# Loading V and storing the output four heads at a time in a grouped-query attention kernel

## The chip, the cores and the metric

The kernel runs on one core of a Trainium2 chip. The metric is the device time of one execution in microseconds. The engines are named as in the profile: PE is TensorE's matrix unit (PEld its weight load), DVE is VectorE, ACT is ScalarE, POOL is GpSimd, and SP is SyncE, which issues every DMA of this kernel. The core's DMA work is done by 16 DMA engines side by side. Each DMA is spread over all 16, and each engine ends its share with an increment of a semaphore, so that a DMA has landed when its semaphore has risen by 16.

## The reference

```python
B, Hq, Hkv, Sq, Sk, D = 16, 32, 8, 16, 2048, 128          # q, k and v are bfloat16

def reference(q, k, v):
    rep = Hq // Hkv                                        # 4 query heads share one K and V
    k = jnp.repeat(k, rep, axis=1)
    v = jnp.repeat(v, rep, axis=1)
    scores = jnp.einsum("bhqd,bhkd->bhqk", q, k) * D ** -0.5
    p = _softmax(scores, axis=-1)
    return jnp.einsum("bhqk,bhkd->bhqd", p, v)
```

There are 16 x 8 = 128 K/V heads. Each has K and V of 2048 x 128 (512 KB each) and serves 4 x 16 = 64 query rows. All of K and V, 134 MB, is read once, and 2 MB of output is written.

## The kernel before, in words

The 128 heads are taken in 64 *pairs* (numbered p, two heads with 128 query rows together, which fill the 128 partitions) and in 32 *quads* (numbered n, two pairs). Every engine runs one straight program written out at build time, and semaphores order the engines against each other.

For each pair the data goes this way. VectorE transposes K in blocks, two instructions a step (`kt`, L355). PE multiplies with the transposed queries into PSUM (`S`, L304 and L260), always for one half of the keys of both pairs of a quad. VectorE scales the scores out of PSUM into `Sneg`, of which there are three buffers, and takes their minimum on the way (L377), and a small instruction (L385) joins the minima of the two halves. ScalarE takes the exponential into `P` and sums the rows (L417). PE transposes `P` (`PT`, L316), ScalarE copies it out of PSUM (L427), and PE multiplies it with V (`PV`, L334 for most pairs, L340 for the rest), four pairs behind the exponential (`PVLAG`). ScalarE divides by the row sums into `Osb` (`norm`, L440 and L444), and VectorE does so for the last five pairs (L398). The two lists `pe_prog` and `act_prog` fix the order on PE and ScalarE.

All transfers go through one queue, in the order of the `sync` program. Its loop counts steps t. A step with an even t asks for K of quad t/2: 2 MB, 16 KB in each partition, into one of three buffers; from the fourth on it waits until the buffer's last transpose is done. Each step asks for V of pair t - 6, or t - 7 from pair 48 on (`VLAG`, `VLATE`): 1 MB, which in each partition is 4 KB from each of two heads, into one of seven buffers. From the eighth on it waits for the PV of the pair seven before (`sem_pv`, L216). Then the step stores the output of pair t - 14 (`SLAG`), 128 rows of 256 bytes, after its normalisation (L235 to L238), from one of eight buffers. V of the last pair comes in two pieces (`LASTV`). Every eighth step a load of Q, 256 KB, comes first. SP executes this in order: a wait before one transfer also holds back those behind it.

The users of those transfers wait as follows. PV of a pair waits for the landing of its V (L322). A normalisation writes its buffer only after the store eight pairs before has landed (L396 on VectorE, L436 on ScalarE). VectorE's first transpose of a quad waits for K (L354).

POOL makes an identity and a mask at the start, through four small tensors of their own (L185 to L198), and later spreads the queries out for their transpose (L176).

Of the kernel before, what the change touches and what calls it, by code (L numbers as in the profile page):

```python
# [5 lines left out]
ACT = mybir.ActivationFunctionType  # L6
# [3 lines left out]
I32 = mybir.dt.int32  # L10

NK = 3
NV = 7
NKT = 2
NS = 3
NPT = 4
NO = 8
NQ = 2
NSTAGE = 3
VLAG = 6  # L20
VLATE = 48
PVLAG = 4
SLAG = 14
QLEAD = 7
# [10 lines left out]
def bass_standalone__gqa_softmax__sampling_kernel(  # L35
# [19 lines left out]
    sb = lambda name, shape, dt: ctx.enter_context(nc.sbuf_tensor(name, shape, dt))  # L55
    sem = lambda name: ctx.enter_context(nc.semaphore(name))

    iota_t = sb("iota_t", [128, 128], I32)
    ident4 = sb("ident4", [128, 128], F32)
    iota_m = sb("iota_m", [128, 4, 4], I32)  # L60
    lo_m = sb("lo_m", [128, 4, 4], F32)
    hi_m = sb("hi_m", [128, 4, 4], F32)
    mask = sb("mask", [128, 4], F32)
    Kn = [sb(f"Kn{i}", [128, 4 * J * 128], BF16) for i in range(NK)]
    Vb = [sb(f"Vb{i}", [128, 2, J, 128], BF16) for i in range(NV)]
    KT = [sb(f"KT{i}", [128, 2 * J * 64], F32) for i in range(NKT)]
    Qn = [sb(f"Qn{i}", [128, 8, 128], BF16) for i in range(NQ)]
    Q4 = sb("Q4", [128, 8, 2, 4, 64], BF16)
# [1 line left out]
    Sneg = [sb(f"Sneg{i}", [128, Sk], F32) for i in range(NS)]  # L70
    P = [sb(f"P{i}", [128, Sk // 2], F32) for i in range(2)]
    PT = [sb(f"PT{i}", [128, J // 2, 128], F32) for i in range(NPT)]
    Osb = [sb(f"O{i}", [128, 128], BF16) for i in range(NO)]
    nhalf = sb("nhalf", [128, 2, NP], F32)
    nbias = sb("nbias", [128, NP], F32)
    rowsum = sb("rowsum", [128, NP], F32)
    rrec = sb("rrec", [128, NP], F32)

    S_ps = ctx.enter_context(nc.psum_tensor("S_ps", [128, Sk], F32))
    ST_ps = ctx.enter_context(nc.psum_tensor("ST_ps", [128, NSTAGE * 512], F32))  # L80
# [1 line left out]

    sem_id = sem("sem_id")
    sem_k = [sem(f"sem_k{i}") for i in range(NK)]
    sem_v = [sem(f"sem_v{i}") for i in range(NV)]
    sem_vl = [sem(f"sem_vl{i}") for i in range(2)]
    sem_q = [sem(f"sem_q{i}") for i in range(NQ)]
    sem_o = [sem(f"sem_o{i}") for i in range(NO)]
# [92 lines left out]
    with nc.Block() as block:  # L181

        @block.gpsimd
        def _(gp):
            gp.iota(iota_m[:, :, :], [[-8, 4], [-32, 4]], base=0, channel_multiplier=1).then_inc(sem_id, 1)  # L185
            gp.iota(iota_t[:, :], [[1, 128]], base=0, channel_multiplier=-1).then_inc(sem_id, 1)
            gp.wait_ge(sem_id, 2)
            gp.tensor_scalar(ident4[:, :], iota_t[:, :], 0.0, None, op0=ALU.is_equal).then_inc(sem_id, 1)
            gp.tensor_scalar(lo_m[:, :, :], iota_m[:, :, :], 0.0, None, op0=ALU.is_ge).then_inc(sem_id, 1)
            gp.tensor_scalar(hi_m[:, :, :], iota_m[:, :, :], 8.0, None, op0=ALU.is_lt).then_inc(sem_id, 1)  # L190
            gp.wait_ge(sem_id, 5)
            gp.tensor_tensor(lo_m[:, :, :], lo_m[:, :, :], hi_m[:, :, :], op=ALU.mult).then_inc(sem_id, 1)
            for x in range(2):
                gp.wait_ge(sem_id, 6 + x)
                a = lo_m[:, :, :] if x == 0 else hi_m[:, :, :]
                w = 2 >> x
                dst = hi_m[:, :, 0:2] if x == 0 else mask[:, :].unsqueeze(2)
                gp.tensor_tensor(dst, a[:, :, 0:w], a[:, :, w:2 * w], op=ALU.add).then_inc(sem_id, 1)  # L198
            gp.wait_ge(sem_id, 8)
            for c in range(1, NQC):  # L200
                gp.wait_ge(sem_st, last_q[c - 1, 3] + 1)
                lay_q(gp, c)

        @block.sync
        def _(sp):
            def load_k(n):
                s = n % NK
                if n >= NK:
                    sp.wait_ge(sem_kt, 4 * (n - NK) + 4)
                sp.dma_start(Kn[s][:, :], kf[n]).then_inc(sem_k[s], 16)  # L210

            def load_v(p):
                s = p % NV
                if p >= NV:
                    sp.wait_ge(sem_pv, p - NV + 1)
                if p < NP - 1:  # L216
                    dst = Vb[s][:, :, :, :].rearrange("a g j d -> a g (j d)")
                    sp.dma_start(dst, vf[:, 2 * p:2 * p + 2, :]).then_inc(sem_v[s], 16)
                    return
                for x, (lo, hi) in enumerate(LASTV):  # L220
                    dst = Vb[s][:, :, lo:hi, :].rearrange("a g j d -> a g (j d)")
                    src = vf[:, 2 * p:2 * p + 2, 128 * lo:128 * hi]
                    sp.dma_start(dst, src).then_inc(sem_vl[x], 16)

            def load_q(c):
                s = c % NQ
                if c >= NQ:
                    sp.wait_ge(sem_q4, 4 * (c - NQ + 1))
                src = qf[1024 * c:1024 * (c + 1), :].rearrange("(a j) d -> a j d", j=8)
                sp.dma_start(Qn[s][:, :, :], src).then_inc(sem_q[s], 16)  # L230

            def store(p):
                s = p % NO
                if p < NP - NLATE:
                    sp.wait_ge(sem_nm, p + 1)  # L235
                else:
                    sp.wait_ge(sem_nl, p - (NP - NLATE) + 1)
                sp.dma_start(of[128 * p:128 * (p + 1), :], Osb[s][:, :]).then_inc(sem_o[s], 16)  # L238

            for t in range(NP + SLAG + 1):  # L240
                for c in range(NQC):
                    if t == max(0, 8 * c - QLEAD):
                        load_q(c)
                if t < NP and t % 2 == 0:
                    load_k(t // 2)
                if 0 <= t - VLAG < VLATE:
                    load_v(t - VLAG)
                if VLATE <= t - VLAG - 1 < NP:
                    load_v(t - VLAG - 1)
                if 0 <= t - SLAG < NP:  # L250
                    store(t - SLAG)
            for s in range(NO):
                sp.wait_ge(sem_o[s], 16 * (NP // NO))

        @block.tensor
        def _(pe):
# [15 lines left out]
            for op in pe_prog:  # L272
# [45 lines left out]
                elif op[0] == "PV":  # L318
                    _, p = op
                    pe.wait_ge(sem_ev, last_p[p, 1] + 1)  # L320
                    if p < NP - 1:
                        pe.wait_ge(sem_v[p % NV], 16 * (p // NV + 1))  # L322
                    if p >= NP - 4:
                        pe.wait_ge(sem_max, 2 * NP)
                    elif p >= 1:
                        pe.wait_ge(sem_nm, p)
                    pt = PT[p % NPT][:, :, :].bitcast(BF16).rearrange("p t (q e) -> p t e q", e=2)
                    for j in range(J):
                        if p == NP - 1:
                            for x, (lo, _) in enumerate(LASTV):  # L330
                                if j == lo:
                                    pe.wait_ge(sem_vl[x], 16)
                        if both_heads(p, NP):
                            ins = pe.matmul(  # L334
                                O_ps[:, 0:256], pt[:, j // 2, j % 2, :], Vb[p % NV][:, :, j, :],
                                start=(j == 0), stop=(j == J - 1),
                            )
                            continue
                        for g in range(2):
                            ins = pe.matmul(  # L340
                                o_ap(p)[64 * g:64 * (g + 1), :],
                                pt[:, j // 2, j % 2, 64 * g:64 * (g + 1)],
                                Vb[p % NV][:, g, j, :],
                                start=(j == 0), stop=(j == J - 1),
                                skip_group_check=True,
                            )
                    ins.then_inc(sem_pv, 1)

        @block.vector
        def _(dve):  # L350
# [41 lines left out]
            for p in range(NP - NLATE, NP):  # L392
                if p == NP - 2:
                    recip(NQD - 1)
                dve.wait_ge(sem_rec, p // 2 + 1)
                dve.wait_ge(sem_o[p % NO], 16 * (p // NO))  # L396
                dve.wait_ge(sem_pv, p + 1)
                dve.tensor_scalar(Osb[p % NO][:, :], o_ap(p), rrec[:, p:p + 1], None, op0=ALU.mult).then_inc(sem_nl, 1)  # L398

        @block.scalar  # L400
        def _(act):
            for op in act_prog:
# [28 lines left out]
                else:  # L431
                    _, p = op
                    act.wait_ge(sem_pv, p + 1)
                    act.wait_ge(sem_rec, p // 2 + 1)
                    if p >= NO:
                        act.wait_ge(sem_o[p % NO], 16 * (p // NO))  # L436
                    if both_heads(p, NP):
                        for g in range(2):
                            rows = slice(64 * g, 64 * (g + 1))
                            ins = act.activation(Osb[p % NO][rows, :], O_ps[rows, 128 * g:128 * (g + 1)], ACT.Copy,  # L440
                                                 scale=rrec[rows, p:p + 1])
                        ins.then_inc(sem_nm, 1)
                        continue
                    act.activation(Osb[p % NO][:, :], o_ap(p), ACT.Copy,  # L444
                                   scale=rrec[:, p:p + 1]).then_inc(sem_nm, 1)


# [26 lines left out]
```

## Time and profile before

| | |
|---|---|
| time, median of three runs | 341.38 us (341.27 to 341.43) |
| the profiled execution | 341.52 us, of which the span of the instructions is 339.7 us |
| DMA | 138.87 MB, mean 409 GB/s over the span |
| busy: PE, DVE, ACT, POOL | 303.7, 305.6, 254.5, 81.4 us |
| V loads: number, size, median from issue to landing | 63 of 1024 KB, 17.2 us (the last pair's two pieces apart) |
| K loads | 32 of 2048 KB, 19.1 us |
| stores | 64 of 32 KB, 16.2 us |
| Q loads | 8 of 256 KB, 14.9 us |

The page of the profile divides the span into 40 slices and shows for each the busy share of every engine in tenths; the DMA row is the mean of 16 DMA engines. The table of the queue counts packets, the single pieces that a DMA engine moves. The list of waits tells which engine stood idle, before which instruction, and what released it. The timeline of SP shows its issuing instructions: the second number is how long one issue took.

### The profile page before, as it was taken

The page shows a single profiled execution, that of the slowest core. Times are in us where ns is not written, and L with a number is a line of the kernel's source. Part 1 is how long each engine was busy: PE and PEld are TensorE (multiplying, and loading weights), DVE is VectorE, ACT ScalarE, POOL GpSimd, SP SyncE. Part 2 cuts the span into 40 slices and gives each one's busy share as a digit, 9 for nine tenths or more (in the row PEclk, how much of TensorE's full clock was granted, in tenths as well). Part 3 has the DMA queues.
Part 4 walks back from the last instruction along what each step waited for, and adds up shares of the span by engine and source line. Part 5 has one row for each costly group of instructions (what it writes and reads, how often), then busy time and mean ns, then how long its engine had stood idle before and what let it go on. Part 6 is the DMA issues. An engine that isn't in the chain of part 4 may idle for free.

```text
span 339.7 us, 7084 instructions
## 1 busy us (share of the span) xinstructions
PE 303.7 (89%) x3040; PEld 182.9 (54%) x2528; DVE 305.6 (90%) x457; ACT 254.5 (75%) x390; POOL 81.4 (24%) x40
## 2 busy tenths in 40 slices
PE   3467799999999999999989999799998999989895
PEld 3113365556655665566546655366555556546464
DVE  1989999999999999999999998899989999999931
ACT  3136878798878878888887887678886887887883
POOL 2840066000920057000750008400093000000000
PEclk9989999999999999999999999899999999999999
DMA  7999999999999999999999999999999999999994
GB/s 297 442 415 420 427 414 412 411 421 425 422 414 413 416 422 426 411 415 414 420 427 418 414 414 416 424 424 421 409 415 418 425 419 424 416 413 414 411 410 162
DMA packets 32688, 138.87 MB, mean 409 GB/s; under 512 B 10896, under 2 KB 11152, under 8 KB 28560
## 3 DMA queue, kind: packets, MB, share of 16 engines
q1 hardware_dynamic: 32656, 138.42, 99.7%
q8 instruction: 22, 0.36, 0.4%
q14 instruction: 10, 0.08, 0.1%
HBM read 136.31 MB, written 2.10 MB: 407 GB/s over the span
## 4 chain that ended last, share of the span: by engine, by line
DMA 35%; PE 35%; DVE 23%; ACT 3%; issue 2%; SPq 1%; ACTq 0%; DVEq 0%
DMA Kn<-in_k_dram 31%; DVE Sneg L377 12%; PE O_ps L334 11%; DVE KT L355 10%; PE S_ps L304 9%; PE S_ps L260 8%; PE ST_ps L316 5%; DMA Vb<-in_v_dram 4%; ACT P L417 2%; PE ST_ps L282 1%; PE O_ps L340 1%; ACT QT L408 1%; ACT O L440 0%; SPq L238 0%; ACT PT L427 0%
## 5 line engine op out<-in xcount | busy, mean ns | idle before, releaser
L355 DVE STREAM_TRANSPOSE KT<-Kn 128x1024 f32<-128x1024 f32 x128 | 151.0, 1218 | 10.9 <-DMA Kn<-in_k_dram 10.8
L377 DVE TENSOR_SCALAR_CACHE_REDUCE Sneg<-S_ps 128x1024 f32<-128x1024 f32 x128 | 150.7, 1209 | 7.9 <-PE S_ps L260 7.0
L417 ACT ACTIVATE P<-Sneg,nbias 128x2048 bf16<-128x2048 f32 x64 | 128.2, 2004 | 16.6 <-DVE nbias L385 15.5
L176 POOL TENSOR_SCALAR Q<-Qn,mask 128x1024 bf16<-128x1024 bf16 x28 | 79.2, 2847 | 175.0 <-DMA Qn<-in_q_dram 95.8
L304 PE MATMUL S_ps<-KT,QT 64*128 64x512 bf16 x512 | 102.7, 390 | 19.7 <-DVE Sneg L377 16.8
L260 PE MATMUL S_ps<-KT,QT 64*128 64x512 bf16 x512 | 102.5, 389 | 0.0
L334 PEld LDWEIGHTS O_ps<-Vb,PT 128*128 128x128 bf16 x672 | 62.6, 98 | 36.7 <-issue 29.8
L334 PE MATMUL O_ps<-Vb,PT 128*128 128x256 bf16 x672 | 81.1, 274 | 1.2 <-issue 1.2
L427 ACT ACTIVATE PT<-ST_ps 128x512 f32<-128x512 f32 x128 | 69.5, 594 | 11.9 <-PE ST_ps L316 10.8
L304 PEld LDWEIGHTS S_ps<-KT,QT 64*128 64x128 bf16 x512 | 27.4, 94 | 87.4 <-issue 75.9
L316 PE MATMUL ST_ps<-ident,P 128*128 128x128 f32 x512 | 67.6, 275 | 3.8 <-ACT P L417 3.7
L440 ACT ACTIVATE O<-O_ps,rrec 64x128 bf16<-64x128 f32 x84 | 30.5, 363 | 42.6 <-PE O_ps L334 42.0
L316 PEld LDWEIGHTS ST_ps<-ident,P 128*128 128x128 f32 x512 | 56.9, 141 | 9.5 <-ACT P L417 8.5
L282 PE MATMUL ST_ps<-ident,Q 128*128 128x128 f32 x128 | 20.4, 291 | 5.5 <-DVE Q L176 5.5
L340 PEld LDWEIGHTS O_ps<-Vb,PT 128*64 128x64 bf16 x576 | 16.7, 110 | 12.9 <-issue 12.9
L408 ACT ACTIVATE QT<-ST_ps 128x512 f32<-128x512 f32 x32 | 19.3, 602 | 5.4 <-PE ST_ps L282 5.4
L340 PE MATMUL O_ps<-Vb,PT 128*64 128x128 bf16 x576 | 19.5, 220 | 1.8 <-issue 1.3
L282 PEld LDWEIGHTS ST_ps<-ident,Q 128*128 128x128 f32 x128 | 16.4, 152 | 5.5 <-issue 5.5
L417 ACT ACTIVATION_READ_ACCUMULATOR P<-Sneg,nbias 128x1 f32 x64 | 12.2, 191 | 0.0
L377 DVE DVE_READ_ACCUMULATOR Sneg<-S_ps 128x1 f32 x128 | 10.6, 83 | 0.0
L444 ACT ACTIVATE O<-O_ps,rrec 128x128 bf16<-128x128 f32 x17 | 6.0, 354 | 3.0 <-PE O_ps L340 3.0
L398 DVE TENSOR_SCALAR O<-S_ps,rrec 128x128 bf16<-128x128 f32 x4 | 1.4, 350 | 6.5 <-PE S_ps L340 6.5
(19 smaller groups left out, 24.4 us busy)
## 6 DMA issues: line engine op xcount, KB each, us to landing
Kn<-in_k_dram SPq DMA_DIRECT2D x32, 2048.0 KB, 19.1
Vb<-in_v_dram SPq DMA_DIRECT2D x63, 1024.0 KB, 17.2
Qn<-in_q_dram SPq DMA_DIRECT2D x8, 256.0 KB, 14.9
out_dram<-O SPq DMA_DIRECT2D x64, 32.0 KB, 16.2
Vb<-in_v_dram SPq DMA_DIRECT2D x1, 768.0 KB, 13.1
Vb<-in_v_dram SPq DMA_DIRECT2D x1, 256.0 KB, 12.8
```

The costliest lines, as they stand in the source:

```text
L176: eng.tensor_scalar(Q4[:, :, :, r, :].rearrange("p j b x -> p (j b) x"), src, mask[:, r:r + 1], None, op0=ALU.mult,).then_inc(sem_q4, 1)
L260: return pe.add_instruction(mybir.InstMatmult(name=nc.get_next_instruction_name(), engine=mybir.EngineType.PE, ins=[pe.lower_ap(rhs), pe.l ...
L282: ins = pe.transpose(dst[:, 128 * j:128 * (j + 1)], src[:, 4 * x + j, b, :], ident4[:, :])
L304: ins = pe.matmul(s_ap, w, x, start=(acc == 0), stop=(acc == 3))
L316: ins = pe.transpose(dst[:, 128 * t:128 * (t + 1)], P[p % 2][:, 128 * x:128 * (x + 1)], ident4[:, :])
L334: ins = pe.matmul(O_ps[:, 0:256], pt[:, j // 2, j % 2, :], Vb[p % NV][:, :, j, :], start=(j == 0), stop=(j == J - 1),)
L340: ins = pe.matmul(o_ap(p)[64 * g:64 * (g + 1), :], pt[:, j // 2, j % 2, 64 * g:64 * (g + 1)], Vb[p % NV][:, g, j, :], start=(j == 0), stop ...
L355: dve.transpose(KT[n % NKT][:, :].rearrange("p (t b g e a) -> p e g t b a", t=J // 4, b=2, g=4, e=2)[:, e], Kn[Q % NK][:, :].bitcast(F32). ...
L377: dve.tensor_scalar(Sneg[p % NS][:, 1024 * x:1024 * (x + 1)].rearrange("p (t a m) -> p t a m", t=4, m=8), S_ps[:, 1024 * y:1024 * (y + 1)] ...
L417: act.activation(P[p % 2][:, :].bitcast(BF16), Sneg[p % NS][:, :], ACT.Exp, bias=nbias[:, p:p + 1], scale=-1.0, accum_out=rowsum[:, p:p + ...
L427: act.activation(PT[p % NPT][:, 4 * h:4 * (h + 1), :].rearrange("p t q -> p (t q)"), stage_ap(u), ACT.Copy,).then_inc(sem_ev, 1)
L440: ins = act.activation(Osb[p % NO][rows, :], O_ps[rows, 128 * g:128 * (g + 1)], ACT.Copy, scale=rrec[rows, p:p + 1])
```

## The change: V and output by quads

V is now loaded by quads for the first 24 quads (`VLATE = 24`, counted in quads): one DMA of 2 MB at the step at which the even pair was asked for, 4 KB from each of four heads in a partition. From quad 24 on V is still asked for by pairs, at the same steps as before. There are four V buffers of a quad in place of seven of a pair. A quad's load waits for the PV of the last pair that used the buffer, which is pair 2n - 7, the pair for which the even half waited before. Each buffer has two semaphores. A load of a quad raises only the first, and PV of both its pairs waits for that; with loads by pairs each pair has its own.

The output of both pairs of a quad is stored by one DMA of 64 KB up to quad 27 (`SLATE = 28`), at the step at which the odd pair was stored; from quad 28 on each pair is stored by itself. There are four output buffers of a quad in place of eight of a pair, and a normalisation of either pair waits for the store of the quad four before.

The larger V buffers take 64 KB of a partition instead of 56. The tensors for the identity and the mask at the start now lie inside the third `Sneg` buffer.

```diff
-NV = 7
+NV = 4
-NO = 8
+NO = 4
-VLATE = 48
+VLATE = 24
+SLATE = 28
...
-    Vb = [sb(f"Vb{i}", [128, 2, J, 128], BF16) for i in range(NV)]
+    Vb = [sb(f"Vb{i}", [128, 4, J, 128], BF16) for i in range(NV)]
...
-    Osb = [sb(f"O{i}", [128, 128], BF16) for i in range(NO)]
+    Osb = [sb(f"O{i}", [128, 2, 128], BF16) for i in range(NO)]
...
+    scratch = Sneg[NS - 1]
+    iota_t = scratch[:, 0:128].bitcast(I32)
...
             def load_v(p):
-                s = p % NV
-                if p >= NV:
-                    sp.wait_ge(sem_pv, p - NV + 1)
+                n, x = divmod(p, 2)
+                s = n % NV
+                if n < VLATE:
+                    if x == 1:
+                        return
+                    if n >= NV:
+                        sp.wait_ge(sem_pv, 2 * (n - NV) + 2)
+                    dst = Vb[s][:, :, :, :].rearrange("a g j d -> a g (j d)")
+                    sp.dma_start(dst, vf[:, 4 * n:4 * n + 4, :]).then_inc(sem_v[s][0], 16)
+                    return
+                sp.wait_ge(sem_pv, p - 2 * NV + 1)
                 if p < NP - 1:
-                    dst = Vb[s][:, :, :, :].rearrange("a g j d -> a g (j d)")
-                    sp.dma_start(dst, vf[:, 2 * p:2 * p + 2, :]).then_inc(sem_v[s], 16)
+                    dst = Vb[s][:, 2 * x:2 * x + 2, :, :].rearrange("a g j d -> a g (j d)")
+                    sp.dma_start(dst, vf[:, 2 * p:2 * p + 2, :]).then_inc(sem_v[s][x], 16)
                     return
...
             def store(p):
-                s = p % NO
+                n, x = divmod(p, 2)
+                s = n % NO
+                if n < SLATE:
+                    if x == 0:
+                        return
+                    sp.wait_ge(sem_nm, p + 1)
+                    dst = of[256 * n:256 * (n + 1), :].rearrange("(x r) d -> r x d", x=2)
+                    sp.dma_start(dst, Osb[s][:, :, :]).then_inc(sem_o[s], 16)
+                    return
...
                     if p < NP - 1:
-                        pe.wait_ge(sem_v[p % NV], 16 * (p // NV + 1))
+                        n, x = divmod(p, 2)
+                        if n < VLATE:
+                            pe.wait_ge(sem_v[n % NV][0], 16 * (n // NV + 1))
+                        else:
+                            pe.wait_ge(sem_v[n % NV][x], 16 * ((n if x == 0 else n - VLATE) // NV + 1))
...
-                dve.wait_ge(sem_o[p % NO], 16 * (p // NO))
+                dve.wait_ge(sem_o[p // 2 % NO], 16 * (p // 2 // NO))
...
-                    if p >= NO:
-                        act.wait_ge(sem_o[p % NO], 16 * (p // NO))
+                    if p >= 2 * NO:
+                        act.wait_ge(sem_o[p // 2 % NO], 16 * (p // 2 // NO))
```

## The prediction

> **What bounds the kernel now.** I read the page's slices first, then the queue table and the DMA issues, then the waits, the chain and the timeline of the queue and of the end. The slices and the queue table:
>
> ```profile
> PE   3467799999999999999989999799998999989895
> DVE  1989999999999999999999998899989999999931
> DMA  7999999999999999999999999999999999999994
> ...
> DMA packets 32688, 138.87 MB, mean 409 GB/s; under 512 B 10896, under 2 KB 11152, under 8 KB 28560
> ...
> q1 hardware_dynamic: 32656, 138.42, 99.7%
> ...
> Vb<-in_v_dram SPq DMA_DIRECT2D x63, 1024.0 KB, 17.2
> ...
> out_dram<-O SPq DMA_DIRECT2D x64, 32.0 KB, 16.2
> ```
>
> Three resources look full, but only the DMA row is full from the first slice to the last but one. Of the 32,656 packets on the queue, 8,192 are 256-byte output rows, 16,128 are 4 KB of V, 4,096 are 16 KB of K, and 2,704 = 169 x 16 are 4-byte completion marks: each of the 169 DMAs (32 K, 63 + 2 V, 8 Q, 64 stores) ends with one mark on each of 16 engines. That is the only count the change alters. (Times of single packets and marks here and below are from the trace's DMA records, which the queue table sums up.)
>
> Next, whether the queue ever runs dry. The sequencer that issues, in the middle:
>
> ```profile
> 244.10 1.27 SPq L210 DMA_DIRECT2D Kn<-in_k_dram  x1
> 245.41 0.44 SPq L218 DMA_DIRECT2D Vb<-in_v_dram  x1
> 245.89 0.47 SPq L238 DMA_DIRECT2D out_dram<-O  x1
> 246.40 6.52 SPq L218 DMA_DIRECT2D Vb<-in_v_dram  x1
> 252.96 1.72 SPq L238 DMA_DIRECT2D out_dram<-O  x1
> ```
>
> A free issue takes 0.4 to 0.5 us; here one takes 6.52 us, and the next starts the moment it ends. [...] The waits and the end:
>
> ```profile
> DVE KT L355 <- DMA Kn<-in_k_dram: 10.8, 11, 3.5
> ...
> 336.20 1.08 PE L340 MATMUL S_ps<-Vb,PT 128*64 128x128 bf16 x32 [0.96 <-DMA Vb<-in_v_dram]
> 337.43 0.35 DVE L398 TENSOR_SCALAR O<-S_ps,rrec 128x128 bf16<-128x128 f32 x1 [1.69 <-PE S_ps L340]
> ```
>
> VectorE waits for K, TensorE waits 0.96 us for the last V. From the completion marks K lands at 191.21, 201.32, 222.49 and 232.61, and its transposes start at 191.2, 201.3, 222.7 and 232.9: VectorE lives hand to mouth on the DMA stream. So the kernel is one ordered stream of packets, and its end is the stream's end on the slowest engine (336.8) plus the last PV, normalise and store.
>
> What a packet costs an engine, from the spacing of packet starts in the trace: 16 KB 607 ns, 4 KB 155 ns, 2 KB 80 ns, 256 B 14 ns, a mark 6 ns (recorded length 9 ns). A quad (K, two V, two stores) is 8 x 607 + 32 x 155 + 16 x 14 + 5 x 6 = 10.07 us; the marks of successive K loads (181.13, 191.21) give 10.08. VectorE needs about 9.4 us for the same quad (its transposes of two successive K loads ended at 100.2 and 109.6, with K well ahead), so the stream is the slower. There is no hidden gap per transfer of more than about 0.01 us.
>
> **The change, part by part.** The sum is made against the profiled execution, 341.52 us (339.7 span and 1.8 around it), which stands 0.14 above the median of 341.38.
>
> **Fewer transfers.** V goes from 65 DMAs to 24 + 15 + 2 = 41, stores from 64 to 28 + 8 = 36; 52 DMAs go, 52 marks on every engine. At the 6 ns spacing that is 0.31 us; at the recorded 9 ns, 0.47. The rest of the quad's measured time over its packets (10.08 to 10.13 against 10.07) is at most 0.06 us over 5 transfers, 12 ns each; two transfers less in 26 quads would then be worth up to 0.6 us more. From below: a mark that overlaps its neighbours wholly is worth 0. I take 0.35 us, nearest to the spacing, and keep 0 to 0.9.
>
> **Packets.** A partition's run in one head is 4 KB in DRAM before and after, and an output row 256 B; so data packets are the same in number and size. Their order changes: K, V, O, V, O becomes K, V, V, O, O. From the marks of the slowest engine, V behind K takes 2.54 us, V behind O 2.42, a store 0.16, K behind O 4.8. V behind V I see only before the first stores, at 24 to 29 us: 2.57. The second store of a pair has no row; by its packets it takes 0.11 to 0.13. A quad in the new order is 4.80 + 2.54 + 2.57 + 0.16 + 0.13 = 10.20 by these, and 10.07 - 0.01 = 10.06 by packet spacing alone; the old order gives 4.80 + 2.54 + 0.16 + 2.42 + 0.16 = 10.08. I take no change, because the packets are the same and the spacing is the nearer row (16 packets of 155 ns make 2.48, whatever stands ahead). For the range I keep +0.12 to -0.02 us in each of 24 quads, +2.9 to -0.5.
>
> **Does a transfer cost more than its packets?** On the empty queue at the end the last store takes 1.45 us from its issue (337.81) to its landing (339.26), but in the full queue a store adds 0.16 us to the stream: the latency is overlapped, and I count only the mark. [...]
>
> **SP.** It issues 52 instructions less, each 0.4 to 0.5 us when free. [...]
>
> **The added waits.** PV of an even pair now waits for the whole 2 MB. Before, PV of the even pairs 24 to 46 starts 0.9 to 2.9 us after the *odd* half has landed (the least, pair 34: PV at 208.00, odd half at 207.11). As the odd half moves ahead of a store (0.16) and sometimes of a Q load (0.54), it lands earlier still, so PV does not wait: 0. If that cover went, S of a later pair, queued behind PV on TensorE, would be late, then VectorE. Normalising an even pair now waits for the store of four heads, four quads back: the smallest margin by today's landings is 1.14 us (pair 62), 2.6 and more up to pair 58. Cost 0. The V load of a quad waits for the PV that its even half waited for, pair 2n - 7; it is free about 10 us before issue. [...]
>
> **The start.** The identity and mask constants move into Sneg's third buffer, which VectorE first writes at its fifth scaled eviction, at 23.9 us; POOL's 2.5 us of set-up lie before K lands at 8.8. Cost 0.
>
> **The end.** Late loads and stores stay as they are. TensorE's 0.96 us wait for the last V covers a stream that ends 0.35 earlier, so the gain reaches the last store whole: 341.52 - 0.35 = 341.17 against the profiled run, 341.38 - 0.35 = 341.03 against the median, 341.0.
>
> **The rivals.**
>
> **R1, the engines are freed of more than marks: faster.** The completion marks show that an engine falls behind by 1.2 to 1.4 us whenever one of the 22 16 KB instruction packets (q8) passes through it; the slowest engine got three (its marks jump at the packets of 34.5, 151.8 and 274.1 us) and lags the fastest by 4.9 us at the end. SP's shorter program may drop one 8 KB instruction fetch (q14, 0.31 us). With 52 x 14 ns = 0.73 for the marks and their surroundings, and with that fetch, 1.04 us: 340.3. For it: the 10.13 us quads. [...]
>
> **R2, four heads in one load read more slowly: slower.** V packets last 161 ns in the mean against a floor of 159; the mean of a single load reaches 165.7 (the one that starts at 297.8). If the walk over four heads, 512 KB apart in DRAM, or V directly behind V, holds the 24 big loads there, that is 24 x 32 x 4.4 ns = 3.4 us, 341.0 + 3.4 = 344.4; it decides from 0.5 ns a packet on. For it: the V loads before the first store, where no store parts them, average 163, which is 2 ns, 1.5 us, and 342.5. Against: the stores stay, only in twos, and from 67 us on V mostly lasts 159 to 163 behind K and behind a store alike; two heads already walk the same way. [...]
>
> **R3, PV or the normalise step waits after all: no change or slower.** It needs the 0.9 us margin to go; a wait of 1 us on TensorE in each quad would still be within VectorE's 0.7 us a quad of slack plus K's buffers, so the time stays near 341.4.
>
> **R4, nothing at all:** marks wholly overlapped, 341.4. [...]
>
> **R5, each transfer pays its latency:** 52 x 1.45 = 75 us; VectorE's 305.6 us of work, 8.8 before it and 3.7 of tail and launch behind it stop the fall at about 318. The back-to-back marks exclude it but for 0.01.
>
> **How the numbers follow.** A change of 0.2% (0.68 us) either way is about what a measurement of this kernel can tell from none. My forecast, 0.1 to 0.68 us gained, has 0.42, R4 0.10 and R3 0.03: together 0.55 within 0.2%. R1 with the good end of the order has 0.27 and R5 0.01: 0.28 faster by more. R2 has 0.17: slower by more. The likeliest time is 341.0. The range goes down to 340.0, past R1's 340.3, and up to 342.4, just under R2's milder form; about 0.06 is left out below and 0.13 above.
>
> **What the profile after would show.** Right: 31,824 packets on the queue (832 fewer), the DMA row as full as now, GB/s in the middle up by a tenth of a percent or so, V issues x24 of 2 MB, TensorE still waiting some 0.6 to 1 us for the last V. Wrong towards faster: K to K under 10.0 us, or a smaller lag of the slowest engine. Wrong towards slower: V packets at 163 ns or more, "PE O_ps <- DMA Vb" among the waits in mid-run, or ACT waiting for a store. The forecast fails if the cost of a transfer on an engine is not in its packets, or if the lag of the slowest engine changes.

## The result and the profile after

The kernel after takes 341.98 us (median of 22 runs) where the kernel before takes 341.40 (22 runs beside it): a ratio of 1.0020, with a 95% interval of 1.0013 to 1.0027. It is 0.58 us slower, and I had forecast a gain of 0.4. The time itself lies in the range I gave, on its other side. The profiled executions stand 0.33 apart, 341.85 against 341.52, their spans 340.1 against 339.7.

The page of the kernel after: the row of the 16 DMA engines, the packet count, the table of the queue, and the DMA issues.

```profile
span 340.1 us, 7030 instructions
...
DMA  7999999999999999999999999999999999999995
...
DMA packets 31856, 138.86 MB, mean 408 GB/s; under 512 B 10064, under 2 KB 10320, under 8 KB 27728
...
q1 hardware_dynamic: 31824, 138.42, 99.9%
...
Vb<-in_v_dram SPq DMA_DIRECT2D x24, 2048.0 KB, 23.3
...
out_dram<-O SPq DMA_DIRECT2D x28, 64.0 KB, 20.3
```

The queue moves the same 138.42 MB in 31,824 packets, 832 fewer: 52 marks on each of 16 engines, as the prediction counted. But the engines are busy for 99.9% of a span that is longer, not for less of it. Fewer packets took more time. The same is seen in the middle of the run, in the view by stretches from 160 to 260 us (the columns are busy times and counts of PE, PEld, DVE, ACT and POOL, the granted clock, the DMA share and GB/s). Before:

```profile
160.00:260.00 100.00, 93.56 (x901) 55.77 (x739) 92.37 (x138) 79.53 (x123) 33.93 (x12) 0.98 1.03 419
```

After:

```profile
160.00:260.00 100.00, 93.79 (x902) 56.16 (x743) 92.62 (x140) 79.21 (x123) 33.70 (x12) 0.98 1.03 418
```

The DMA share is the same and the rate falls from 419 to 418 GB/s, where I had looked for a small rise. The sequencer that issues, at the same place as before:

```profile
244.96 0.66 SPq L213 DMA_DIRECT2D Kn<-in_k_dram  x1
246.02 0.37 SPq L224 DMA_DIRECT2D Vb<-in_v_dram  x1
246.45 7.55 SPq L251 DMA_DIRECT2D out_dram<-O  x1
254.05 1.73 SPq L213 DMA_DIRECT2D Kn<-in_k_dram  x1
```

Issues are drawn out as before (6.52 us there): that of a store lasts 7.55 us here, where V's just ahead of it took 0.37. From the list of waits (us in total, times, longest):

```profile
DVE KT L378 <- DMA Kn<-in_k_dram: 11.0, 12, 3.6
```

From the timeline of the end:

```profile
336.54 1.08 PE L363 MATMUL S_ps<-Vb,PT 128*64 128x128 bf16 x32 [0.86 <-DMA Vb<-in_v_dram]
337.76 0.35 DVE L421 TENSOR_SCALAR O<-S_ps,rrec 128x128 bf16<-128x128 f32 x1 [1.59 <-PE S_ps L363]
```

VectorE's waits for K add up to 11.0 us against 10.8. No wait of PE for V and none of ACT for a store has joined the list in mid-run. The full list has one new row, VectorE idle for 2.7 us before a normalisation (L421), put down to a store. It shows no wait for a store: it is the normalisation of pair 61, at 333.78 us, and the store that it needed, of quad 26, had landed at 329.21 by the completion marks. What landed just before 333.78 was part of a later store on the same semaphore. POOL's idle time is only put down otherwise (125.3 us to Q instead of 95.8, 52.5 to PE instead of 79.2). The last V lands at 337.13 instead of 336.77, PE begins its last PV 0.34 later, and the last normalise comes 0.33 later. So the whole loss is in the stream.

Two numbers from the trace's DMA records are used below. One is the *stream time*: the completion mark of K of quad 26 less that of quad 6, each as the mean over the 16 engines, so that the lag of a single engine enters by a sixteenth. It covers twenty quads with 40 V loads of a pair; the first store follows K of quad 7, so 19 of the quads have stores, 38 of a pair. The other is the mean recorded length of the 4 KB packets in the first and second half of a quad's V (quads 4 to 23). The records do not name the engine, so these packets are counted off in the order of their starts, 256 to a half. In before and after the marks of one K lie 0.6 to 3.4 us apart in these quads, 1.8 and more from quad 5 on, so neighbouring halves mix, and the true differences may be larger. The stream time went from 207.41 to 207.92 us. The halves went from 161.7 and 160.6 ns to 161.7 and 164.0: the half that used to stand behind a store and now stands behind V became slower by 3.4 ns a packet.

### The profile page after: what moved, and what is told of

It reads as the page before. It is cut to its first block, busy times and chain, and to the rows that moved or that the text cites. A ratio compares the mean times of both kernels' runs of the same rounds, so it can differ in the third digit from the quotient of the medians.

```text
span 340.1 us, 7030 instructions
## 1 busy us (share of the span) xinstructions
PE 305.4 (90%) x3040; PEld 183.5 (54%) x2528; DVE 305.7 (90%) x457; ACT 254.6 (75%) x390; POOL 81.4 (24%) x40
## 3 DMA queue, kind: packets, MB, share of 16 engines
q1 hardware_dynamic: 31824, 138.42, 99.9%
## 4 chain that ended last, share of the span: by engine, by line
DMA 35%; PE 33%; DVE 22%; SPq 4%; ACT 3%; issue 2%; ACTq 0%; DVEq 0%
DMA Kn<-in_k_dram 32%; DVE Sneg L400 12%; PE O_ps L357 10%; DVE KT L378 10%; PE S_ps L323 8%; PE S_ps L279 8%; PE ST_ps L335 5%; DMA Vb<-in_v_dram 4%; SPq L241 2%; ACT P L440 2%; PE ST_ps L301 1%; SPq L251 1%; PE O_ps L363 1%; ACT QT L431 1%; ACT PT L450 0%
## 5 line engine op out<-in xcount | busy, mean ns | idle before, releaser
L179 POOL TENSOR_SCALAR Q<-Qn,mask 128x1024 bf16<-128x1024 bf16 x28 | 79.2, 2846 | 177.8 <-DMA Qn<-in_q_dram 125.3
L335 PE MATMUL ST_ps<-ident,P 128*128 128x128 f32 x512 | 68.5, 277 | 3.6 <-ACT P L440 3.4
L335 PEld LDWEIGHTS ST_ps<-ident,P 128*128 128x128 f32 x512 | 57.7, 142 | 9.9 <-ACT P L440 8.9
L421 DVE TENSOR_SCALAR O<-S_ps,rrec 128x128 bf16<-128x128 f32 x4 | 1.4, 351 | 6.4 <-PE S_ps L363 3.8
```

Of the source, the lines that this page charges most:

```text
L179: eng.tensor_scalar(Q4[:, :, :, r, :].rearrange("p j b x -> p (j b) x"), src, mask[:, r:r + 1], None, op0=ALU.mult,).then_inc(sem_q4, 1)
L335: ins = pe.transpose(dst[:, 128 * t:128 * (t + 1)], P[p % 2][:, 128 * x:128 * (x + 1)], ident4[:, :])
```

## The experiments

In the strings below K is a 2 MB load, V a load of a pair and VV one of a quad, O a store of a pair and OO one of a quad, o a store of 64 rows, all in the order of the queue within one quad. The theories at the start were that the place of V in the order makes it slow (ORDER), that 2 MB loads are slow as such (SIZE), or that the buffers and waits are to blame. STORE put the loss on the 64 KB store. MARKS says that each completion mark costs its 6 ns. HIDE came later: a store is partly hidden among loads, and two stores with a load between them are hidden better than two together. The diffs of e4, e8, e10, e11, v1 and v2 are against e1, those of e5, e6 and v3 against e3, that of e9 against e2, the others against after. Lines that only fit the waits to the new numbers of DMAs are left out of them.

| run | order | time, us | ratio to before (95%) | stream time, us | V halves, ns |
|---|---|---|---|---|---|
| before | K V O V O | 341.40 | | 207.41 | 161.7, 160.6 |
| after | K VV OO | 341.98 | 1.0020 (1.0013, 1.0027) | 207.92 | 161.7, 164.0 |
| after, again | K VV OO | 341.98 | 1.0018 (1.0006, 1.0030) | 208.00 | 161.7, 163.5 |
| e1 | K V O V O | 341.42 | 0.9999 (0.9990, 1.0008) | 207.46 | 161.6, 160.5 |
| e2 | K VV O O | 341.91 | 1.0013 (1.0004, 1.0022) | 208.04 | 161.6, 163.4 |
| e3 | K V V OO | 342.02 | 1.0015 (1.0006, 1.0024) | 207.97 | 161.4, 162.9 |
| e4 | K O V O V | 341.94 | 1.0014 (1.0005, 1.0023) | 207.49 | 159.4, 160.3 |
| e5 | V K V OO | 341.79 | 1.0012 (1.0003, 1.0020) | 207.69 | 160.3, 162.0 |
| e6 | K V V | 338.16 | 0.9908 (0.9893, 0.9923) | 205.17 | 162.9, 164.3 |
| e7 | K VV | 338.13 | 0.9902 (0.9889, 0.9916) | 205.16 | 163.1, 164.2 |
| e8 | K O V o V o | 341.62 | 1.0006 (0.9997, 1.0015) | 207.15 | 159.6, 160.4 |
| e9 | K O VV O | 341.86 | 1.0021 (1.0007, 1.0035) | 207.61 | 159.8, 163.0 |
| e10 | K V oo V oo | 341.71 | 1.0010 (1.0002, 1.0019) | 207.66 | 161.6, 160.4 |
| e11 | K, then o and V of one head four times | 341.35 | 0.9998 (0.9989, 1.0006) | 207.22 | 159.4, 159.8 |
| v1 | K V V O O | 342.16 | 1.0017 (1.0008, 1.0026) | 208.11 | 161.5, 163.2 |
| v2 | before's, V by single heads | 341.61 | 1.0005 (0.9996, 1.0013) | 207.47 | 161.0, 160.1 |
| v3 | K V OO V | 341.95 | 1.0015 (1.0006, 1.0023) | 207.70 | 162.0, 159.7 |

The kernels that share an order, before and e1, and the two profiles of after, differ by 0.05 and 0.08 us in the stream time, and by up to 0.5 ns in a V half. Differences of 0.2 us and more are read; what is worked out from smaller ones below is rough.

**e1: the buffers and semaphores of after, with the loads and stores of before.**

```diff
-SLATE = 28
+VQ = 0
+SLATE = 0
...
-                if n < VLATE:
+                if n < VQ:
...
-                act.wait_ge(sem_o[p // 2 % NO], 16 * (p // 2 // NO))
+                act.wait_ge(sem_o[p // 2 % NO], 32 * (p // 2 // NO))
```

> The change with every load of V and every store back at its pair and at its old step; what stays of it is the four quad-sized V buffers, the four output buffers and the constants inside Sneg. All theories: this is the time before, 341.4 us within 0.2, and V in quads 4 to 23 has a mean packet of 161.7 ns behind K and 160.6 ns behind a store, as before. If it is at 342.0 instead, the buffers or their waits cost the 0.6 us and not the transfers.

It is level with before in time (0.9999) and in the stream (207.46). Fewer buffers, a normalisation that waits for both stores of a quad, and constants inside a `Sneg` buffer cost nothing that shows. The wait of PV for a whole 2 MB is not in e1; it is the lists of waits of after and e2 that show no wait of PE for V before the last one. The loss is in the DMAs.

**e2: V by quads, the stores by pair.** Two stores in a row follow each 2 MB load.

```diff
-SLATE = 28
+SLATE = 0
```

> V by quads as in the change, but each pair's output is stored by itself, at its old step; the queue's order in a quad becomes K, 2 MB of V, store, store. Theory ORDER (V that follows V with no store between them is read more slowly, 164.0 ns a packet in the second half against 160.6): 342.1 us, 0.17 more than the change for the 28 marks that come back, second half at 164. Theory SIZE (the 2 MB load over four heads is itself slower): the same 342.1. Theory STORE (the 64 KB store is what costs): 341.3, second half at 161.

**e3: V by pairs, the stores by quads.** There is no 2 MB load of V at all, but the second V stands behind the first.

```diff
+VQ = 0
...
-                if n < VLATE:
+                if n < VQ:
```

> V by pairs of 1 MB at the old steps, output of two pairs in one 64 KB store; the order in a quad becomes K, V, V, store, and no load is larger than before. ORDER: the second V of a quad at 164 ns, 342.0 to 342.2 us. SIZE: second V at 161 ns, 341.2 us. STORE: 342.0 us with the second V at 161 ns.

The queue and the issues of e3:

```profile
q1 hardware_dynamic: 32208, 138.42, 99.9%
...
Vb<-in_v_dram SPq DMA_DIRECT2D x63, 1024.0 KB, 20.0
...
out_dram<-O SPq DMA_DIRECT2D x28, 64.0 KB, 17.0
```

Both halves of the change lose as much as the whole: 208.04 and 207.97 in the stream, 341.91 and 342.02 in time. In e3 all V loads are 1 MB (x63), so SIZE falls. In e2 no store is larger than before, and STORE had given it 341.3, so the 64 KB store is not needed for the loss either. What e2 and e3 have in common with after is only that V follows V and that the stores stand together.

**e4: a store ahead of each V.** All DMAs as in before, the store of each step moved ahead of that step's V.

```diff
+                if 0 <= t - SLAG < NP:
+                    store(t - SLAG)
                 if 0 <= t - VLAG < 2 * VLATE:
                     load_v(t - VLAG)
...
-                if 0 <= t - SLAG < NP:
-                    store(t - SLAG)
```

> Loads and stores by pairs as in the kernel before, but in each step the store stands ahead of the V load; the order in a quad becomes K, store, V, store, V, so that both V loads stand behind a store and K stands behind V. ORDER: the first V falls from 161.7 to about 160.6 ns, the second stays, K may rise by a few ns in 611: 340.9 to 341.4 us. SIZE and STORE: no change, 341.4 us, V as before (161.7 and 160.6).

The first V is faster, as ORDER said (159.4 ns), the second as it was within the scatter (160.3), and the kernel is not faster. K, which now stands behind V, is read at 617.6 ns a packet instead of 614.8, and the stream time is that of before (207.49). What V gains behind a store, K that no longer stands behind one loses for the most part: by the recorded lengths V gains 0.83 us in twenty quads and K loses 0.67. The time, 341.94, is neither what ORDER expected nor the 341.4 of the other theories; it is taken up below.

**e5: K between the two V loads, one store of four heads at the end.** The stores are by quads in the first twenty quads.

```diff
+                early = t % 2 == 0 and 0 <= t - VLAG < 2 * VLATE
+                if early:
+                    load_v(t - VLAG)
                 if t < NP and t % 2 == 0:
                     load_k(t // 2)
-                if 0 <= t - VLAG < 2 * VLATE:
-                    load_v(t - VLAG)
+                if early:
+                    load_v(t - VLAG + 1)
```

> V by pairs of 1 MB, the output of two pairs in one 64 KB store for the first 20 quads, and for the first 24 quads the V load of the even pair is asked for ahead of K instead of behind it: V, K, V, store. No V stands behind a V, the stores stand together as in the change. ORDER: the first V at 160 to 161 ns, the second, behind K, at 161 to 162 ns, and the time of the kernel before less 20 marks (0.12 us), 341.1 to 341.5 us. STORE (a 64 KB store is what costs, whatever stands beside it): 341.8 to 342.1 us with V at 161 ns.

V does not follow V here, and half of the stream's loss is left, 207.69; the time, 341.79, is at the lower end of what STORE gave. ORDER alone does not carry it. That it need not be the size of the store is known from e2.

**e6 and e7: the first 28 quads are not stored at all,** with V by pairs (e6) and by quads (e7).

```diff
                 if n < SLATE:
-                    if x == 0:
-                        return
-                    sp.wait_ge(sem_nm, p + 1)
-                    dst = of[256 * n:256 * (n + 1), :].rearrange("(x r) d -> r x d", x=2)
-                    sp.dma_start(dst, Osb[s][:, :, :]).then_inc(sem_o[s], 16)
                     return
```

> V by pairs at the old steps; the output of the first 28 quads is computed and normalised but not stored, so 56 stores of a pair leave the queue and V stands behind V in every quad. Packets alone would make it 56 x 0.118 = 6.6 us shorter than before, 334.8 us. ORDER: V rises to about 163 and 164 ns for lack of stores between, 28 x 16 x (1.3 + 3.4) ns = 2.1 us come back, 336.9 us (336.3 to 337.3). If the stores do nothing for the loads (SIZE): V stays at 161.7 and 160.6, 334.8 us.

> As the one before, without the stores of the first 28 quads, but V of the first 24 quads in one 2 MB load each. ORDER: nothing parts the two halves in either, so this one is 24 marks (0.14 us) faster or level: 336.8 us, within 0.3 of the other. SIZE: it is slower than the other by 0.6 to 1.1 us, with only its second halves at 164 ns.

The span and the queue of e6:

```profile
span 336.0 us, 7026 instructions
...
q1 hardware_dynamic: 24592, 136.58, 99.4%
```

And of e7:

```profile
span 336.4 us, 7002 instructions
...
q1 hardware_dynamic: 24208, 136.58, 99.3%
```

Two things follow. The 384 packets between the two are 24 marks on each engine, and the stream times are 205.17 and 205.16: without stores, a mark fewer behind a V load is worth nothing that shows. And 56 stores cost before only 341.4 - 338.2 = 3.2 us, and 207.41 - 205.17 = 2.24 for the 38 in the stream time, 0.059 each. By the spacing of its packets (8 of 14 ns and a mark of 6) a store takes 0.118. So half of it is hidden, and the records show where. Both theories missed the time of e6: SIZE had 334.8, and ORDER 336.9, which is still 1.3 us short of what came back. Over the whole run V is read at 163.6 ns and K at 618.3 without stores, and at 161.3 and 614.8 with them. Loads run faster behind a store here (e4's first V: 159.4 ns, against 161.7 behind K). From here on the theory was HIDE: what a store costs depends on the loads it stands between.

**e8: three stores in a quad, each before or behind a V.** The odd pair's store is cut into 64 and 64 rows.

```diff
+                p = t - SLAG
+                if 0 <= p < NHALF:
+                    store(p, 0, 128 if p % 2 == 0 else 64)
                 if 0 <= t - VLAG < 2 * VLATE:
                     load_v(t - VLAG)
...
+                if 0 <= p < NHALF and p % 2 == 1:
+                    store(p, 64, 128)
```

> All by pairs; the even pair's store stands ahead of its V, and the odd pair's store is cut into two of 64 rows, one ahead of its V and one behind it (first 27 quads): K, store, V, half, V, half. Each V stands behind a store as in the kernel with stores first, and K too. 27 marks more, 0.16 us. ORDER alone: V at 159.4 and 160.3 ns, K at 614 ns, 341.0 us. LAG (what an engine gains in packet length is lost again where it lags behind the others, as in the kernel with stores first, where V fell to 159.4 and 160.3 ns and the time was 341.94): 341.7 to 342.2 us.

The stream is the shortest with all stores in it, 207.15, in spite of 19 more marks. The time, 341.62, is not: nothing is gained over before that its interval would show. It lies between the 341.0 of ORDER and the 341.7 or more of LAG, the theory named only here. In the profile the last V lands 0.37 us earlier than in before in the mean over the engines (334.10 against 334.47), and 0.10 earlier on the slowest one (336.67 against 336.77).

**e9: V by quads, with one store ahead of it and one behind.** It differs from e2 only in the place of one 32 KB store of each quad.

```diff
+                first = t - VLAG < 2 * VLATE and t % 2 == 0
+                if 0 <= t - SLAG < NP and first:
+                    store(t - SLAG)
                 if 0 <= t - VLAG < 2 * VLATE:
                     load_v(t - VLAG)
...
-                if 0 <= t - SLAG < NP:
+                if 0 <= t - SLAG < NP and not first:
                     store(t - SLAG)
```

> V of the first 24 quads in one 2 MB load as in the kernel after, but the stores by pair, one ahead of the V load and one behind it: K, O, VV, O. Beside the kernel after two things differ: the stores don't stand together, and they are two. HIDE (a store costs less when a V load parts it from the next store, and two V loads in a row cost nothing by themselves): the mean landing of K26 less K6 is 207.3 to 207.6 us as before (207.41), not 207.9, and the time 341.3 to 341.6; the second half of the 2 MB load is read at about 164 ns a packet, the first at 159 to 160. ORDER (a V load directly behind V is read more slowly, and that is what the change lost): 16 packets at 159.5 and 16 at 164 against 161.7 and 160.6 before, +0.02 us in a quad, so 207.7 and 341.7. SIZE (a 2 MB load is slow by itself): 207.9 or more and 341.9. Where the slowest engine lags behind the mean more than before, the time stands up to 0.4 us above these, and the mean landing decides.

Moving that store took 0.43 us out of the stream (208.04 to 207.61), with the sizes and the marks unchanged. But 0.20 above before is left, which lies between what HIDE and ORDER gave; the time, 341.86, is above both. The first half of V is read at 159.8 ns behind the store, the second at 163.0 behind V.

**e10: before, with each of the first 56 stores cut into two of 64 rows,** one right behind the other.

```diff
-                sp.dma_start(of[128 * p:128 * (p + 1), :], Osb[s][:, x, :]).then_inc(sem_o[s], 16)
+                for lo, hi in ((0, 64), (64, 128)) if p < NHALF else ((0, 128),):
+                    sp.dma_start(of[128 * p + lo:128 * p + hi, :], Osb[s][lo:hi, x, :]).then_inc(sem_o[s], 16)
```

> The order of before, all loads by pair, and each of the first 56 stores cut into two DMAs of 64 rows, one right behind the other: 56 completion marks more on each engine, and the same packets at the same places. MARKS (a mark takes the 6 ns by which it stands apart from the next packet): 56 x 6 = +0.34 us, so 341.75, and 40 x 6 = +0.24 in the mean landing of K26 less K6, 207.65. FREE (a mark lies under the packets behind it): 341.4 and 207.4. LATENCY (each DMA costs something of its own beyond its mark, at least 0.02 us): +1.1 us or more, 342.5.

MARKS was right here: 207.66 and 341.71 against 207.65 and 341.75. So close a hit is luck, since profiles of one order differ by 0.05 to 0.08 us. 38 store DMAs more cost 0.25 us of stream, about 6 ns each.

**e11: the opposite of the change.** V by single heads, with half a store ahead of each load.

```diff
+                    for g in range(2):
+                        if 0 <= q < NHALF:
+                            store(q, 64 * g, 64 * g + 64)
+                        dst = Vb[s][:, 2 * x + g, :, :].rearrange("a j d -> a (j d)")
+                        sp.dma_start(dst, vf[:, 2 * p + g, :]).then_inc(sem_v[s][x], 16)
```

> The opposite of the change: V in 512 KB loads of one head, and half a store (64 rows) ahead of each of them: K, o, V, o, V, o, V, o, V. 56 store DMAs and 63 V DMAs more than before. HIDE: each small store stands between two loads and is hidden at least as well as with three pieces in a quad, 207.15 or less in the mean landing of K26 less K6 (before 207.41), and the time 341.2 to 341.6 by how far the slowest engine lags. MARKS: 119 marks more, +0.7 us, 342.1. If single DMAs cost something that big ones save, this is the kernel that shows it: 342 or more.

The page of e11:

```profile
span 339.4 us, 7256 instructions
...
q1 hardware_dynamic: 34560, 138.43, 99.9%
...
Vb<-in_v_dram SPq DMA_DIRECT2D x126, 512.0 KB, 14.5
...
out_dram<-O SPq DMA_DIRECT2D x112, 16.0 KB, 14.0
```

With 2,736 packets more than after, all of them marks, the span is 0.7 us shorter than after's, and the time is level with before. The stream is 0.19 us shorter (HIDE had asked for a little more, 207.15 or less). V is read at 159.4 and 159.8 ns. This is the clearest sign that the number of DMAs was the smaller matter.

**The kernel after once more,** beside e9 to e11.

> The kernel after once more, beside the three: 341.9 to 342.0, and 207.9 in the mean landing of K26 less K6, with the second half of V at 164 ns a packet. A mean landing of 207.5 or less would take the ground from all that is read of that number, since it would then move by itself from run to run by as much as the orders are said to.

It was 341.98 and 208.00, so the stream time does not wander by the 0.5 us that is read from it.

**v1: order alone.** All DMAs of before; only the even pair's store of the first 28 quads is moved behind the second V.

```diff
+TOGETHER = 56
...
-                if 0 <= t - SLAG < NP:
+                if 0 <= t - SLAG < TOGETHER:
+                    if t % 2 == 1:
+                        store(t - SLAG - 1)
+                        store(t - SLAG)
+                elif 0 <= t - SLAG < NP:
                     store(t - SLAG)
```

> All DMAs of before, by pair, and only the even store of the first 28 quads moved behind the second V load: K, V, V, O, O. ORDER or HIDE (the places of the DMAs are the whole loss): the mean landing of K26 less K6 is 207.9 to 208.1 us, the second half of V 163 to 164 ns a packet, and the time 341.8 to 342.0. If it is 207.4 to 207.5 and 341.4, order is not the cause, and the loss lies in the merging of the DMAs after all.

The page of v1:

```profile
span 340.4 us, 7082 instructions
...
DMA packets 32688, 138.87 MB, mean 408 GB/s; under 512 B 10896, under 2 KB 11152, under 8 KB 28560
...
q1 hardware_dynamic: 32656, 138.42, 100.0%
...
Vb<-in_v_dram SPq DMA_DIRECT2D x63, 1024.0 KB, 19.3
...
out_dram<-O SPq DMA_DIRECT2D x64, 32.0 KB, 14.9
```

The counts of packets, loads and stores are those of before, and it is as slow as after or a little slower: 342.16 us, 0.71 above the 341.45 of before beside it, and 208.11 in the stream, 0.70 above before. The order is the whole loss in the stream. Merging the DMAs, the only other thing in the change that touches the stream, gave 0.1 to 0.2 of it back by the stream time; the two ratios to before (1.0017 and 1.0020) don't part v1 from after.

**v2: marks alone.** Before's order, each V load cut into two of one head.

```diff
+                    for g in range(2):
+                        dst = Vb[s][:, 2 * x + g, :, :].rearrange("a j d -> a (j d)")
+                        sp.dma_start(dst, vf[:, 2 * p + g, :]).then_inc(sem_v[s][x], 16)
```

> The order of before, and each V load of a pair but the last cut into two of one head, one right behind the other: 63 completion marks more on each engine, all behind 4 KB packets, and the stores as before. MARKS (6 ns each wherever they stand): 40 x 6 = +0.24 in the mean landing of K26 less K6, 207.65, and 63 x 6 = +0.38 in the time, 341.77. LOAD MARKS FREE (a mark behind a load costs nothing, what the halved stores lost was the marks of writes or the cut of a store): 207.4 and 341.4.

40 marks more behind V loads changed the stream by 0.06 us, within the scatter; the time, 341.61, lies between the two theories, and its interval includes no change. With e7 (20 fewer, 0.01) and the step from v1 to e2 (20 fewer, 0.07) a V load's mark is worth between 0 and 4 ns.

**v3: the stores together, but between the two V loads.**

```diff
+                between = t % 2 == 1 and 0 <= t - SLAG < 2 * SLATE
+                if between:
+                    store(t - SLAG)
                 if 0 <= t - VLAG < 2 * VLATE:
                     load_v(t - VLAG)
```

> V by pair, the store of four heads in one as in the kernel after, but between the two V loads of a quad: K, V, OO, V. HIDE (stores that stand together are hidden worse than stores with a load between them, wherever they stand): 207.8 to 208.0 in the mean landing of K26 less K6, 341.8 to 342.0. ORDER (V behind V is what is slow): no V stands behind V here, so 207.4 less 20 marks, 207.3 to 207.4, and 341.3.

Its 207.70 lies between the theories once more, 0.29 above before. Both are half right, and the four corners add up within the scatter. Stores together, V parted (v3): +0.29, and with its 19 merged stores at 6 to 7 ns put back, about +0.42. V behind V, stores parted (e9): +0.20 with at most 0.07 to put back. Both at once (v1): +0.70, where the sum is 0.62 to 0.69. One quad later (K of quad 27 less that of quad 7, where all twenty quads have stores) the three are +0.23, +0.13 and +0.64. So the stores' standing together is the larger part, 0.35 to 0.43 us; V behind V is 0.13 to 0.28 (the upper end is v1 less v3), and by itself at the edge of what is read here.

The two causes may be one. With three loads and two stores in a quad, stores that stand together also leave one more load directly behind a load. Counting these loads gives none in e8, one in before, two in v3 and v1, with 207.15, 207.41, 207.70 and 208.11 in the stream. But e4 and e9 have one as well (207.49, 207.61), so it would matter which load it is. This is read from the table; no run tests it alone.

**What stays open.** The time is set by the slowest of the 16 engines, and the mean over them explains it only to about 0.4 us. In e4, e9 and v3 the time stands 0.5 above before while the stream explains 0.1 to 0.3. Their profiles tell more: in every profile of the table the execution's time is the last landing of V on the slowest engine plus 4.70 to 4.78 us, in e8's alone plus 4.89. Against before (336.77) this landing is 0.43 later in e4, 0.19 in e9 and 0.30 in v3. In e4 the mean over the engines is level with before there (334.53 against 334.47), and the slowest engine comes 2.68 us after the mean instead of 2.30. So the loss of this execution is lag alone. Whether the order makes the lag is not shown, since the two profiles of after also differ in it (2.02 and 2.27). In e9 and v3 the medians stand another 0.12 and 0.13 above their profiled executions. What makes a load faster behind a store was not looked into; only that it is.

## Why the prediction was wrong

**What bounds the kernel: right.** One ordered stream, the queue busy for 99.7 and 99.9% of the span, the end set by the last V. The PE wait of 0.86 us at the end lies in the 0.6 to 1 named, the packets are 31,824 to the last one, and the 0.36 us by which the last V is late reaches the last normalise as 0.33.

**Packets, "I take no change": the step that failed.** The prediction had three rows: V behind V 2.57 us on the slowest engine against 2.42 behind a store; the V packets before the first store at 163 ns against 161; and the spacing of 155 ns, "whatever stands ahead". It took the last, which gave zero, and kept 0.12 us a quad as an end. v1 measures the term: 0.70 us in the 19 quads with stores, 0.037 a quad, between the two. Over 24 to 28 quads that is an estimated loss of 0.9 to 1.0 us; less what the merging gives back (next paragraph), 0.6 to 0.9, beside the 0.58 measured. Spacing was the wrong row because it was read in the old order alone, as the mean of V behind K and V behind a store. In the runs with V by pairs and quads these are different numbers: 159.4 to 160.6 ns behind a store, 161.4 to 163.1 behind K, 162.9 to 164.3 behind V. In v1 the V halves alone give 16 x (163.2 - 160.6 + 161.5 - 161.7) = 38 ns a quad, 0.77 us in 20, beside the 0.70 measured. This sum doesn't hold everywhere. Where K stands behind V (e4, v3) K pays too: in e4 V and K together give -0.16 us, where the stream has +0.08. In e11 they give -0.86, where the stream has -0.19.

**Fewer transfers, -0.35: right in sign, too large.** From v1 to after, with 39 DMAs fewer in the stream time, the stream falls by 0.11 to 0.19 (the two profiles of after). The 6 ns is about right for stores (e10: 0.25 for 38; v1 to e3: 0.14 for 19) and too much for loads of V (v2, e7). With 28 stores at 6 and 24 loads at 0 to 4 ns the term would have been 0.17 to 0.26. Whether the 6 ns of a store are those of its mark or of its cut, e10 doesn't tell.

**Latency, SP, the added waits, the start: right, all at nothing.** e1 holds the buffers, the constants and the wait for a quad's stores at 0.02 us, and the list of waits shows none of PV for a whole 2 MB. SP's shorter program moved no end that the profile shows. No run shows what draws an issue out to 6.52 or 7.55 us, so the zeros for SP and for the late loads were a guess of mine; what the runs show is that with 52 issues fewer the queue is no less busy (99.9% against 99.7) and VectorE waits for K as before (11.0 us against 10.8).

**The rivals.** R1 did not come: the instruction packets are as many as before (22 and 10), and the engines were freed of nothing more. R2 had two mechanisms in one sentence. The walk over four heads in one load is excluded by e3 and e7. V directly behind V is what happened, and its sign, V packets at 163 ns or more, is there at 164.0. It was priced at 2 and at 4.4 ns on every V packet of 24 quads, 342.5 and 344.4. Over the whole run V became 1.3 ns slower (161.3 to 162.6), because only the second halves slowed; the missing marks gave some of the time back. (K is 1.0 ns a packet faster in the first profile of after, 613.8 against 614.8, but 615.0 in the second.) R4 holds for the V loads' marks. R3 saw no wait. What no rival had was the stores standing together (v3): the case against R2, that "the stores stay, only in twos", was taken for a comfort, and it was the larger part of the loss.

## What to carry to other kernels

In this stream, busy for 99.9% of the span, the order of DMAs weighed more than their number (v1 lost 0.70 us, and merging gave 0.1 to 0.2 back): look in the records at what a packet lasts behind each kind of neighbour before you call a reordering free. Here small stores spread between large loads were half hidden (0.059 us of 0.118), and grouping them undid some of that; merging DMAs was worth 6 to 7 ns for each store and 0 to 4 for each load of V. When a change both merges and moves, look for a row in which the new neighbours already stand together, however short that stretch of the trace is, and trust its sign before its size: here it gave 0.12 us a quad, and v1 measured 0.037.

## What the runs showed that I had not expected

A pair's store, 32 KB in rows of 256 bytes, costs the stream 0.059 us in before and 0.118 by its own packets; in after it is (207.92 - 205.16) / 38 = 0.073. Loads without any store beside them were slower per packet (V 163.6 against 161.3 ns, K 618.3 against 614.8) and the effect hangs on the next neighbour in the queue, down to single 32 KB stores (e9: V at 159.8 ns behind one, 163.0 behind V). And 119 further DMAs (e11: 512 KB loads, 16 KB stores) left the time where it was and the stream 0.19 us shorter, so their places gained at least what their marks cost.
